# Hash-bucketed attention followed by two MLPs on one core: another order for the first pairs of heads, filler matmuls, late copies, and a last block stored tile by tile

## The chip, the cores and the metric

One core of one Trainium2 chip runs the whole kernel as one program. The metric is the device time of that core in microseconds. Times of single executions agree to about 0.1%; a time given here is the median of a few executions, and the profile comes from one more execution, with a time of its own.

The engines are called as the profile calls them: PE is TensorE (matmuls; PEld its weight loads), DVE is VectorE, ACT is ScalarE, POOL is GpSimd, SP is SyncE, whose queue issues nearly all the DMAs here. Each engine works through its own instructions in the order in which the program gives them, and waits on semaphores for the others.

## The reference

Inputs are `q`, `k`, `v` of shape (2, 8, 768, 64), a projection `proj` (64, 6) and two pairs of MLP weights, (512, 2048) and (2048, 512), all float32 (float64 in memory for the weights).

```
q_bits, k_bits = (q @ proj > 0), (k @ proj > 0)        # 6 bits a row: its bucket
scores = q @ k^T / 8;  scores[bucket(q) != bucket(k)] = -1e9
attn = softmax(scores);  x = attn @ v                  # 16 heads, 768 x 768 each
x = relu(x @ w_in)^2 @ w_out                           # 1536 tokens, 512 -> 2048 -> 512
g = h * tanh(softplus(h)), h = x @ w2_in;  out = g @ w2_out
```

Every float32 product is made of three products of float32r halves (high*high, high*low, low*high), so each matmul below comes in threes or with a second operand that carries the low halves.

## The kernel before

**Attention.** The 16 heads form 8 pairs. One step j (96 of them, N = 96, 12 to a pair, PER = 12) handles 128 queries of one head against all 768 keys. A step has, on PE: four score matmuls (`scores`, L365 and L367), six transposes of the exponentials (`transpose`, L392) and four matmuls with v for the group of three steps before (`pv`, L421). On DVE: `clamp` (L373, reads the scores from PSUM and takes the maximum) and `lower` (L409, low half of the transposed exponentials). On ACT: `exponent` (L382) and `upper` (L405, high half). Step j of the loop (L551 to L596) issues `scores(j+2)`, `exponent(j+1)`, `lower(j-1)`, `transpose(j)`, `clamp(j+2)`, `upper(j)`, a part of `pv`, in that order.

**PSUM.** `ps2` has three slots of two banks, taken in turn by scores, transposes and bits; `ps1` has two slots of one bank for the accumulators of `pv`. So scores and transposes of a step wait until DVE has emptied the slot they follow. The program puts the slots of `ps2` at banks 0, 4, 2 in turn and those of `ps1` at 6 and 7. After the attention the MLPs' pools take the same banks: hidden tiles (`psh`) at 4, 7, 6, 5 in turn, accumulators (`pacc`) at 0, 3, 2, 1.

**The next pair** is prepared inside the steps of the present one, by a plan (L483 to L499): `load` (q and k from memory), `split_q`, `split_k`, `split_v` on POOL (L311 to L346), `place_q`, `place_k` (three DMAs each, L321 and L339), and once a pair eight matmuls that make the hash bits (`bits_split`, L286), at the end of the step in `bits_at`. In the next step ACT negates one half of the bits (L291), DVE compares (L294), POOL scales (L295), and `place_bits` puts them below q and k by four DMAs (L304, L305). Calls of the plan run at the head of their step; the DMAs among them all go through SP's queue, one behind the other, each with its waits.

**Taking a group out.** After three steps of `pv` the accumulator is copied by ACT (`unstack`): for the first head of a pair to `hi` (L434), for the second to `both` (L439), a buffer of which there is one. Two DMAs (L442, L443, `place`) take `both` away a step later, behind all other calls of that step. `broadcast` (L450) copies the reciprocal sums out of PSUM (L453) and spreads them by DMAs (L461), `finish` (L465) on POOL adds and scales into `xf`. The first pair runs head by head, so that its two `both` come three steps apart; in the other pairs they come six steps apart.

**Weights.** `weights` (L86) converts float64 weights piece by piece. A piece is a fetch (512 KB), an absolute value (L117 on ACT in the attention), clamp and shift on DVE (L121, L122), two ORs on DVE (L124, L126) and two instructions on POOL (L127, L128). `next(conv)` takes one stage of it; `conv_at` names the steps that take one, at their end: 21 stages, five pieces, in the attention.

**The turn to the MLPs** (L597 to L626): the last sums are transposed into `rT`, the last `lower`, the ACT copies of `rT` and of accumulator 30, four `split` of the first block of tokens (L615 on ACT, L616 on DVE), twelve matmuls of the last `pv`, the last `unstack`.

**The MLPs** run as 8 weight groups by 3 blocks of 512 tokens by 4 chunks: `hidden` (L642 to L644, twelve matmuls), activation, and five steps later `down` (L688 to L696, twelve matmuls). `down` of the second MLP adds chunk fi to four accumulators (one for 128 tokens each); after the fourth chunk `collect` adds all four to `tot` on DVE (L710) and stores each by a DMA on SP (L713).

Of the kernel before, what the change touches and what calls it, by code (L numbers as in the profile page):

```python
# [17 lines left out]
P = 128  # L18
# [10 lines left out]
LAG = 5  # L29

WARM = 3

F64_LOW = 3.4332275390625e-05
# [4 lines left out]
def lsh_attention_relu2_mish_kernel(ctx, tc, qT, kT, vP, proj, w_in, w_out, w2_in, w2_out, out):  # L38
# [47 lines left out]
    def weights():  # L86
# [16 lines left out]
        for k, (i, nm, _, c) in enumerate(pieces):  # L103
# [11 lines left out]
            mu = m.bitcast(U32)  # L115
            if loaded[-1] == EXP_SET:
                nc.scalar.activation(m, hf, AF.Abs)  # L117
            else:
                nc.vector.scalar_tensor_tensor(m, hf, -1.0, hf, ALU.mult, ALU.max)
            yield  # L120
            nc.vector.tensor_scalar(m, m, F64_LOW, F64_HIGH, ALU.max, ALU.min)  # L121
            nc.vector.tensor_scalar(mu, mu, 3, 0x3FFFFFF8, ALU.logical_shift_left, ALU.bitwise_and)  # L122
# [25 lines left out]
    pm = early.enter_context(tc.tile_pool(name="pm", bufs=3))  # L148
    ps2 = early.enter_context(tc.tile_pool(name="ps2", bufs=3, space=PSUM))

# [208 lines left out]
    def scores(j):  # L359
        p, half, hh, t = seq[j]  # L360
        QA, QBt, KA, KBt = heads[p, hh]
        q0 = half * H2 + t * P
        ps = sc[j] = ps2.tile([P, 1024], F32, tag="ps2", name="s")
        for c0, c1 in ((0, 512), (512, S)):
            nc.tensor.matmul(ps[:, c0:c1], QA[:, q0:q0 + P], KA[:, c0:c1], start=True, stop=False)  # L365
        for c0, c1 in ((0, 512), (512, S)):
            nc.tensor.matmul(ps[:, c0:c1], QBt[:, q0:q0 + P], KBt[:, c0:c1], start=False, stop=True)  # L367
# [44 lines left out]
    def pv(g, n):  # L412

        p, half, hh, _ = seq[g * QT]
        if n == 0:
            accs[g] = ps1.tile([P, H2], F32, tag="ps1", name="acc")
# [8 lines left out]
    def unstack(g, j):  # L425
# [10 lines left out]
        else:  # L436
            hi, lo = hl[p, half]
            both = xt.tile([P, H2], F32, tag="both", name="both", bufs=1)
            nc.scalar.activation(both, acc, AF.Copy)  # L439
# [4 lines left out]

            at(j + 1, place)
            at(j + 4 + 2 * (j == N), lambda: finish(p, half))
# [32 lines left out]

    def at(j, f):  # L480
        calls.setdefault(j, []).append(f)

    bits_at = {}  # L483
    for p in range(NP - 1):
        o, n = p * PER, p + 1
        if p == 0:
            plan = ((3, split_q, (n,)), (4, split_k, (n,)), (5, place_q, (n, 0)), (6, place_k, (n, 0)),
                    (6, place_q, (n, 1)), (7, place_k, (n, 1)), (8, place_bits, (n, 0)), (8, place_bits, (n, 1)),
                    (8, split_v, (n,)), (8, load, (n + 1, "q_r")), (8, load, (n + 1, "k_r")), (11, load_v, (n + 1,)))
            bits_at[o + 6] = n  # L490
        else:
            plan = ((1, place_k, (n, 0)), (2, load, (n + 1, "q_r")), (3, load, (n + 1, "k_r")), (3, split_v, (n,)),
                    (7, place_bits, (n, 0)), (7, place_q, (n, 1)), (8, place_bits, (n, 1)), (8, place_k, (n, 1)),
                    (10, load_v, (n + 1,)))
            bits_at[o + 4] = n
# [4 lines left out]

    conv_at = [5, 6, 6, 8, 10] + [b for b in bits_at if b > PER for _ in range(2)] + [N - PER + m for m in (1, 4, 6, 8)]

# [43 lines left out]
    load(1, "q_r")  # L546
    load(1, "k_r")
    load_v(1)
    split_proj()
    waiting, bits, sums = None, None, None  # L550
    for j in range(N):  # L551
# [4 lines left out]
        if j + 1 < N:  # L556
            exponent(j + 1)
            sums = next((k for k, last in ends.items() if last == j + 1), None)
            if sums is not None:
                add_tiny(sums)  # L560
        if bits is not None:
            bits[0]()
        if waiting is not None:
            unstack(waiting, j)
            waiting = None
        if j:
            lower(j - 1)
        if bits is not None:
            bits[1]()
            bits = None  # L570
        if j == 1:
            head_qbits(1, 0, S, qb1)
        done = next(iter(r6s), None)
        transpose(j, r6s.get(done))
        if j + 2 < N:
            clamp(j + 2)
        if sums is not None:
            nc.vector.reciprocal(tiny[sums], tiny[sums])
            if j + 2 < N:
                r6s[sums] = tiny[sums]  # L580
            sums = None
        upper(j)
        if done is not None:
            del r6s[done]
            broadcast(*done, pts[j][:2 * QT, S:S + P], j)
        g, n = divmod(j, QT)
        if g:
            pv(g - 1, n)
            if n == QT - 1:
                waiting = g - 1  # L590
        if j == 0:
            qb1 = head_bits(1, 0, 0, S)
        if j in bits_at:
            bits = bits_split(bits_at[j])
        for _ in range(conv_at.count(j)):
            next(conv)  # L596
    for f in calls.pop(N, ()):  # L597
        f()
    ps = ps2.tile([P, 1024], F32, tag="ps2", name="rT")
    done = seq[N - 1][:2]  # L600
    r6 = tiny[done]
    nc.tensor.transpose(ps[:2 * QT, 0:P], r6, ident)
    lower(N - 1)
    broadcast(*done, ps[:2 * QT, 0:P], N)
    unstack(waiting, N)
    early.close()

# [10 lines left out]
    xs = {}  # L618
    split((0, 0), xf[0])
    for n in range(QT):  # L620
        pv(N // QT - 1, n)
    unstack(N // QT - 1, N)
# [77 lines left out]
    def collect(i, blk, acc):  # L700
# [13 lines left out]
        if layer == 0 and g == G - 1:  # L714
            split((1, blk), tot[blk])

    def retire(i, blk, fi, gh, gl):
        if fi == 0:
            acc[:] = [
# [68 lines left out]
```

## Time and profile before

| | |
|---|---|
| median of 3 runs | 762.97 us (762.72 to 763.20) |
| the profiled execution's own time | 762.05 us |
| its span | 759.9 us |
| PE busy | 745.8 us, 98% of the span |
| DVE, ACT, POOL busy | 534.5, 358.0, 263.9 us |
| chain that ended last | PE 86%, DMA 4%, DVE 3%, ACT 2%, POOL 2%, issue 2% |

The span goes from the first to the last recorded instruction; 2.15 us of the execution lie around it. A chain is followed back from the last instruction to whatever released it. In a row of the timeline the columns are start, length, engine, line, operation, operands, count, and in brackets the idle time before it with what ended it.

### The profile page before, as it was taken

To read this page: it belongs to the slowest core of one execution; us is meant where nothing else is said; L and a number is where in the kernel's file an instruction comes from. 1 tells how busy PE (TensorE), PEld (TensorE's weight loads), DVE (VectorE), ACT (ScalarE), POOL (GpSimd) and SP (SyncE) were. 2 spreads that over 40 slices of the span, in tenths; PEclk is the share of its full clock that TensorE was granted. 3 is DMA by queue.
4 is the path that set the end of the run, shared out by engine and by line. 5 is a ranking of instruction groups with operands and counts; after the bars stand their busy time and mean duration, and the time that the engine had idled before them with its cause. 6 is when DMAs were issued, how large, how long until landed. Compare 5 with 4: busy or idle time off the path is not lost.

```text
span 759.9 us, 10509 instructions
## 1 busy us (share of the span) xinstructions
PE 745.8 (98%) x3742; PEld 635.5 (84%) x3742; DVE 534.5 (70%) x859; ACT 358.0 (47%) x640; POOL 263.9 (35%) x261
## 2 busy tenths in 40 slices
PE   8889999999999999999999999999999999999997
PEld 4779999999998888888888888888888888888886
DVE  8878988988997966566566688978454767566223
ACT  6878889889897443423233213333223121212120
POOL 9464555655223433232232232224223222232100
PEclk9999999999999999999999999999999999999999
DMA  5775696678423122122121122112212111120013
GB/s 145 196 207 157 167 232 158 167 203 193 108 71 92 56 84 82 57 69 70 56 84 55 56 68 67 60 56 84 84 55 81 59 56 56 56 83 28 1 55 111
DMA packets 28956, 72.69 MB, mean 96 GB/s; under 512 B 5048, under 2 KB 10264, under 8 KB 28904
## 3 DMA queue, kind: packets, MB, share of 16 engines
q1 hardware_dynamic: 28824, 72.01, 33.5%
q8 instruction: 30, 0.49, 0.3%
q14 instruction: 22, 0.18, 0.1%
q10 hardware_dynamic: 80, 0.00, 0.0%
HBM read 46.14 MB, written 3.19 MB: 65 GB/s over the span
## 4 chain that ended last, share of the span: by engine, by line
PE 86%; DMA 4%; DVE 3%; ACT 2%; POOL 2%; issue 2%; SPq 0%; DVEq 0%; ACTq 0%; POOLq 0%
PE h L642 11%; PE h L644 11%; PE h L643 11%; PE pT L392 6%; PE acc L421 6%; PE acc L688 6%; PE acc L689 6%; PE acc L690 6%; PE acc L696 6%; PE acc L695 6%; PE acc L694 6%; PE s L367 3%; PE s L365 3%; DVE pl L409 1%; ACT ph L405 1%
## 5 line engine op out<-in xcount | busy, mean ns | idle before, releaser
L643 PE MATMUL h<-xs,wi 128*128 128x512 f32 x384 | 149.4, 389 | 0.0
L644 PE MATMUL h<-xs,wi 128*128 128x512 f32 x384 | 149.4, 389 | 0.0
L642 PE MATMUL h<-xs,wi 128*128 128x512 f32 x384 | 149.4, 389 | 0.0
L668 ACT ACTIVATE g<-h 128x512 f32<-128x512 f32 x48 | 28.7, 598 | 188.7 <-PE h L644 172.0
L409 DVE TENSOR_TENSOR pl<-pT,ph 128x768 fp32r<-128x768 f32 x96 | 91.7, 956 | 20.1 <-ACT ph L405 13.4
L652 ACT ACTIVATE r<-h 128x512 f32<-128x512 f32 x48 | 28.7, 598 | 153.3 <-PE h L644 153.3
L127 POOL TENSOR_SCALAR wo<-cv 128x512 fp32r<-128x512 f32 x32 | 29.4, 918 | 194.3 <-DVE cv L126 178.9
L382 ACT ACTIVATE e<-e,nm 128x768 f32<-128x768 f32 x96 | 89.8, 936 | 6.0 <-DVE e L373 5.5
L673 DVE TENSOR_TENSOR gl<-g,gh 128x512 fp32r<-128x512 f32 x48 | 35.9, 748 | 80.6 <-ACT gh L670 80.6
L373 DVE TENSOR_SCALAR_CACHE_REDUCE e<-s 128x768 f32<-128x768 f32 x96 | 91.0, 947 | 0.9 <-PE s L367 0.8
L654 DVE TENSOR_TENSOR s<-r 128x512 f32<-128x512 f32 x48 | 38.8, 808 | 70.2 <-ACT r L652 70.2
L405 ACT ACTIVATE ph<-pT 128x768 fp32r<-128x768 f32 x96 | 77.7, 809 | 18.2 <-PE pT L394 10.1
L644 PEld LDWEIGHTS h<-xs,wi 128*128 128x128 f32 x384 | 72.1, 188 | 15.1
L642 PEld LDWEIGHTS h<-xs,wi 128*128 128x128 f32 x384 | 72.1, 188 | 14.9
L643 PEld LDWEIGHTS h<-xs,wi 128*128 128x128 f32 x384 | 72.0, 188 | 14.8
L392 PE MATMUL pT<-ident,e 128*128 128x128 f32 x576 | 79.1, 273 | 3.6 <-DVE pl L409 3.2
L127 POOL TENSOR_SCALAR wi<-cv 128x512 fp32r<-128x512 f32 x32 | 27.3, 854 | 147.5 <-DVE cv L126 147.5
L392 PEld LDWEIGHTS pT<-ident,e 128*128 128x128 f32 x576 | 66.3, 140 | 11.2 <-ACT r L386 1.9
L688 PE MATMUL acc<-gh,wo 128*128 128x512 f32 x192 | 74.7, 389 | 0.0
L689 PE MATMUL acc<-gl,wo 128*128 128x512 f32 x192 | 74.7, 389 | 0.0
L690 PE MATMUL acc<-gh,wo 128*128 128x512 f32 x192 | 74.7, 389 | 0.0
L694 PE MATMUL acc<-wo,gh 128*128 128x512 f32 x192 | 74.7, 389 | 0.0
(111 smaller groups left out, 1413.8 us busy)
## 6 DMA issues: line engine op xcount, KB each, us to landing
stg<-in_w_in_dram SPq DMA_DIRECT2D x32, 512.0 KB
stg<-in_w_out_dram SPq DMA_DIRECT2D x32, 512.0 KB
KA<-kh SPq DMA_DIRECT2D x28, 192.0 KB
v_r<-in_vP_dram SPq DMA_DIRECT2D x8, 384.0 KB
rb<-rd SPq DMA_DIRECT2D x32, 96.0 KB
out_dram<-tot SPq DMA_DIRECT2D x12, 256.0 KB
q_r<-in_qT_dram SPq DMA_DIRECT2D x7, 384.0 KB
k_r<-in_kT_dram SPq DMA_DIRECT2D x7, 384.0 KB
```

The costliest lines, as they stand in the source:

```text
L373: nc.vector.tensor_scalar(e, ps[:, 0:S], MASKED, None, ALU.min, ALU.min, accum_out=nm)
L382: nc.scalar.activation(e, e, AF.Exp, bias=nm, scale=-1.0, accum_out=ssums[p, half][:, c:c + 1])
L392: nc.tensor.transpose(ps[:, c * P:(c + 1) * P], e[:, c * P:(c + 1) * P], ident)
L405: nc.scalar.activation(ph, v, AF.Copy)
L409: nc.vector.tensor_tensor(pl, v, b32(ph), ALU.subtract)
L642: nc.tensor.matmul(h, w[:, 0, fi, cs], xs[:, 0, c, :], start=c == 0, stop=False)
L643: nc.tensor.matmul(h, w[:, 0, fi, cs], xs[:, 1, c, :], start=False, stop=False)
L644: nc.tensor.matmul(h, w[:, 1, fi, cs], xs[:, 0, c, :], start=False, stop=c == PPB - 1)
L688: nc.tensor.matmul(y, w[:, 0, fi, cs], gh, start=fi == 0, stop=False)
L689: nc.tensor.matmul(y, w[:, 0, fi, cs], gl, start=False, stop=False)
L690: nc.tensor.matmul(y, w[:, 1, fi, cs], gh, start=False, stop=fi == FC - 1)
L694: nc.tensor.matmul(o, gh[:, qs], w[:, 0, fi, :], start=fi == 0, stop=False)
```

## The change

- The plan of the first pair is re-ordered: the loads of pair 2 go from step 8 to step 4, bits from step 6 to 5, `place_k(1, 0)` and both `place_bits` one step earlier, `place_k(1, 1)` one later, `load_v` from 11 to 9. For the second pair (p = 1) the loads go from steps 14 and 15 to 16 and 17.
- `conv_at` is another list of the same 21 stages, one of which (the first fetch) runs before step 0. In a step the stage now comes after `lower(j-1)` and ahead of compare, transposes and `clamp`.
- For pieces 1 to 4 the absolute value and its clamp are three POOL instructions, in place of one on ACT and one on DVE.
- `scores(0)` gets two matmuls with a tile of zeros (`FILL`) between its first and second pair of matmuls.
- `place` of `both` goes to the head of its step's calls.
- The end of the attention: `clamp(95)` comes one step earlier (ahead of `lower(92)`), the copies out of accumulators 29 and 30 come after the loop, between and behind the `split`s; the last sums are made on DVE; the copy of the transposed sums (now `rp`) comes after all `split`s; the last `pv` accumulates in a slot of `ps2`, which therefore stays open until the end of the attention.
- The last block's `down` of the second MLP: chunks are kept, and after the fourth each 128-token tile gets its twelve matmuls in a row, its addition and its DMA; the last tile is done in two halves of 256 columns, the second half stored through ACT's queue.

```diff
+EARLY = 5
+FILL = 2
...
-            if loaded[-1] == EXP_SET:
+            if 0 < k < EARLY:
+                nc.gpsimd.tensor_scalar(m, hf, 0.0, -2.0, ALU.min, ALU.mult)
+                nc.gpsimd.tensor_tensor(m, m, hf, ALU.add)
+                nc.gpsimd.tensor_scalar(m, m, F64_LOW, F64_HIGH, ALU.max, ALU.min)
+            elif loaded[-1] == EXP_SET:
                 nc.scalar.activation(m, hf, AF.Abs)
...
-            nc.vector.tensor_scalar(m, m, F64_LOW, F64_HIGH, ALU.max, ALU.min)
+            if not 0 < k < EARLY:
+                nc.vector.tensor_scalar(m, m, F64_LOW, F64_HIGH, ALU.max, ALU.min)
...
-    ps2 = early.enter_context(tc.tile_pool(name="ps2", bufs=3, space=PSUM))
+    ps2 = late.enter_context(tc.tile_pool(name="ps2", bufs=3, space=PSUM))
...
+        for _ in range(FILL * (j == 0)):
+            nc.tensor.matmul(ps[:, 0:H2], zero[:, 0:P], zero, start=False, stop=False)
...
-            both = xt.tile([P, H2], F32, tag="both", name="both", bufs=1)
+            if g < N // QT - 1:
+                both = xt.tile([P, H2], F32, tag="both", name="both", bufs=1)
+            else:
+                both = b32(pt.tile([P, KT, H2], F32R, tag="ph", name="both")[:, 0, :])
...
-            at(j + 1, place)
+            at(j + 1, place, j < N)
...
-    def at(j, f):
-        calls.setdefault(j, []).append(f)
+    def at(j, f, first=False):
+        c = calls.setdefault(j, [])
+        c.insert(0 if first else len(c), f)
...
-            plan = ((3, split_q, (n,)), (4, split_k, (n,)), (5, place_q, (n, 0)), (6, place_k, (n, 0)),
-                    (6, place_q, (n, 1)), (7, place_k, (n, 1)), (8, place_bits, (n, 0)), (8, place_bits, (n, 1)),
-                    (8, split_v, (n,)), (8, load, (n + 1, "q_r")), (8, load, (n + 1, "k_r")), (11, load_v, (n + 1,)))
-            bits_at[o + 6] = n
+            plan = ((3, split_q, (n,)), (4, split_k, (n,)), (4, load, (n + 1, "q_r")), (4, load, (n + 1, "k_r")),
+                    (5, place_q, (n, 0)), (5, place_k, (n, 0)), (6, place_q, (n, 1)), (7, place_bits, (n, 0)),
+                    (7, place_bits, (n, 1)), (8, place_k, (n, 1)), (8, split_v, (n,)), (9, load_v, (n + 1,)))
+            bits_at[o + 5] = n
         else:
-            plan = ((1, place_k, (n, 0)), (2, load, (n + 1, "q_r")), (3, load, (n + 1, "k_r")), (3, split_v, (n,)),
+            m = 2 if p > 1 else 4
+            plan = ((1, place_k, (n, 0)), (m, load, (n + 1, "q_r")), (m + 1, load, (n + 1, "k_r")), (3, split_v, (n,)),
...
-    conv_at = [5, 6, 6, 8, 10] + [b for b in bits_at if b > PER for _ in range(2)] + [N - PER + m for m in (1, 4, 6, 8)]
+    conv_at = [4, 6, 6]
+    for p in range(1, NP - 1):
+        conv_at += [p * PER + m for m in ((4, 6) if p % 2 else (4, 5))]
+    conv_at += [N - PER - 4, N - PER - 3] + [N - PER + m for m in (2, 3, 6)]
...
     load(1, "k_r")
+    next(conv)
     load_v(1)
...
-        if waiting is not None:
+        if waiting is not None and j < N - QT:
             unstack(waiting, j)
             waiting = None
+        if j == N - 3:
+            clamp(j + 2)
+        if j == N - 1:
+            done = seq[j][:2]
+            r6 = sm.tile([P, 2 * QT], F32, tag="r6", name="r6", bufs=2)
+            nc.vector.tensor_scalar(r6, ssums.pop(done), 1e-9, None, ALU.add)
+            nc.vector.reciprocal(r6, r6)
         if j:
             lower(j - 1)
+        for _ in range(conv_at.count(j)):
+            next(conv)
         if bits is not None:
             bits[1]()
             bits = None
...
-        if j + 2 < N:
+        if j + 3 < N:
             clamp(j + 2)
...
-        for _ in range(conv_at.count(j)):
-            next(conv)
-    for f in calls.pop(N, ()):
-        f()
-    ps = ps2.tile([P, 1024], F32, tag="ps2", name="rT")
-    done = seq[N - 1][:2]
-    r6 = tiny[done]
-    nc.tensor.transpose(ps[:2 * QT, 0:P], r6, ident)
+    rp = ps2.tile([P, 1024], F32, tag="ps2", name="rT")[:2 * QT, 0:P]
+    nc.tensor.transpose(rp, r6, ident)
     lower(N - 1)
-    broadcast(*done, ps[:2 * QT, 0:P], N)
-    unstack(waiting, N)
+    accs[N // QT - 1] = ps2.tile([P, 1024], F32, tag="ps2", name="acc")[:, 0:H2]
+    for n in range(QT):
+        pv(N // QT - 1, n)
     early.close()
...
-    split((0, 0), xf[0])
-    for n in range(QT):
-        pv(N // QT - 1, n)
+    split((0, 0), xf[0], 0, 2)
+    unstack(waiting, N - 1)
+    for f in calls.pop(N):
+        f()
+    split((0, 0), xf[0], 2)
+    unstack(N // QT - 2, N)
+    broadcast(*done, rp, N)
     unstack(N // QT - 1, N)
...
+    def last(blk, kept):
+        w = W[2 * G - 1, "o"]
+        nt = TB // P
+        for t in range(nt):
+            qs = slice(t * P, (t + 1) * P)
+            o = pacc.tile([P, DM], F32, tag="acc", name="acc")
+            n = 1 + (t == nt - 1)
+            for h in range(n):
+                cs = slice(h * DM // n, (h + 1) * DM // n)
+                for fi, (gh, gl) in enumerate(kept):
+                    nc.tensor.matmul(o[:, cs], gh[:, qs], w[:, 0, fi, cs], start=fi == 0, stop=False)
+                    nc.tensor.matmul(o[:, cs], gh[:, qs], w[:, 1, fi, cs], start=False, stop=False)
+                    nc.tensor.matmul(o[:, cs], gl[:, qs], w[:, 0, fi, cs], start=False, stop=fi == FC - 1)
+                x = tot[blk][:, t, cs]
+                nc.vector.tensor_tensor(x, x, o[:, cs], ALU.add)
+                r0 = blk * TB + t * P
+                (nc.scalar if h else nc.sync).dma_start(out=out[r0:r0 + P, cs], in_=x)
...
     def retire(i, blk, fi, gh, gl):
+        if (i, blk) == (2 * G - 1, NBLK - 1):
+            kept.append((gh, gl))
+            if fi == FC - 1:
+                last(blk, kept)
+            return
```

## Rows read from the trace of the kernel before

**Rows 1.** Waits of PE: what waited for what, total us, times, longest.
```profile
PE pT L392 <- DVE pl L409: 3.2, 6, 1.6
PE bits L286 <- POOL xf L474: 3.2, 1, 3.2
PE s L367 <- DVE QB L262: 1.2, 1, 1.2
PE s L365 <- DVE pl L409: 0.6, 1, 0.6
```

**Rows 2.** Timeline of PE, steps 39 to 41: start, length, engine, line.
```profile
106.89 0.82 PE L392 MATMUL pT<-ident,e 128*128 128x128 f32 x6
...
108.94 0.82 PE L392 MATMUL pT<-ident,e 128*128 128x128 f32 x6
...
110.30 0.51 PE L286 MATMUL bits<-qh,pwr 128*112 128x512 f32 x2
...
111.70 0.51 PE L365 MATMUL s<-KA,QA 128*128 128x512 f32 x2
...
113.09 0.85 PE L392 MATMUL pT<-ident,e 128*128 128x128 f32 x6 [0.54 <-DVE pl L409]
```

**Rows 3.** Timelines of PE, ACT, DVE and POOL, 26 to 37 us.
```profile
26.06 0.82 PE L392 MATMUL pT<-ident,e 128*128 128x128 f32 x6
...
31.27 0.84 PE L392 MATMUL pT<-ident,e 128*128 128x128 f32 x6 [1.60 <-DVE pl L409]
...
28.66 0.67 ACT L117 ACTIVATE cv<-stg 128x512 f32<-128x512 f32 x1 [0.94 <-DMA stg<-in_w_in_dram]
...
34.92 1.76 DVE L124 SCALAR_TENSOR_TENSOR cv<-stg,cv 128x512 uint32<-128x512 uint32 x1
...
34.28 1.85 POOL L346 TENSOR_TENSOR vs<-v_r,vs 128x768 fp32r<-128x768 f32 x1
```

**Rows 4.** Groups by line and form: count, busy us, mean ns, idle before.
```profile
L124 DVE SCALAR_TENSOR_TENSOR cv<-stg,cv 128x512 uint32<-128x512 uint32 x64 | 45.0, 704 | 1.0
...
L128 POOL TENSOR_TENSOR wi<-cv,wi 128x512 fp32r<-128x512 f32 x32 | 43.4, 1356 | 2.7
...
L208 PE MATMUL zeros<-zero 128*128 128x384 f32 x6 | 4.1, 857 | 1.3 <-DVE zero L184 1.3
...
L222 PE MATMUL bits<-k,pw 128*76 128x512 f32 x4 | 2.0, 592 | 0.0
```

**Rows 5.** Timelines of PE, ACT, SP and POOL, 40 to 60 us.
```profile
51.02 0.82 PE L392 MATMUL pT<-ident,e 128*128 128x128 f32 x6
...
59.16 1.14 PE L392 MATMUL pT<-ident,e 128*128 128x128 f32 x6
...
53.42 0.49 ACT L439 ACTIVATE both<-acc 128x384 f32<-128x384 f32 x1 [3.90 <-DMA lo<-both]
...
48.95 0.82 SPq L443 DMA_DIRECT2D lo<-both  x1
...
40.40 1.12 POOL L311 TENSOR_SCALAR qh<-q_r 128x768 fp32r<-128x768 f32 x1 [4.27 <-DMA q_r<-in_qT_dram]
```

**Rows 6.** Stretch 58 to 60 us: busy time of each engine, PEclk, DMA share, GB/s.
```profile
58.00:60.00 2.00, 2.00 (x10) 1.80 (x10) 1.79 (x3) 0.81 (x1) 0.00 (x0) 0.55 0.44 160
```

**Rows 7.** Timelines of ACT and PE, 229 to 234 us.
```profile
229.81 1.64 ACT L405 ACTIVATE ph<-pT 128x768 fp32r<-128x768 f32 x2
231.44 0.27 ACT L453 ACTIVATE rs<-rT 6x128 f32<-6x128 f32 x1
...
231.98 2.18 ACT L615 ACTIVATE xs<-xf 128x512 fp32r<-128x512 f32 x4
...
233.70 0.39 PE L642 MATMUL h<-xs,wi 128*128 128x512 f32 x1
```

**Rows 8.** Timeline of DVE from 752 us.
```profile
754.11 2.73 DVE L710 TENSOR_TENSOR tot<-tot,acc 128x512 f32<-128x512 f32 x4 [8.15 <-PE acc L696]
```

**Rows 9.** DMA rate in 40 equal slices of 753 to 760 us.
```profile
GB/s 0 0 0 0 0 0 0 0 0 0 0 0 0 0 0 257 410 386 351 363 386 386 351 387 398 374 375 375 398 410 339 47 0 0 0 0 0 0 0 0
```

More of the change, by code (lines that the diff above doesn't have):

```diff
@@ L414, in pv @@
         p, half, hh, _ = seq[g * QT]
-        if n == 0:
+        if n == 0 and g not in accs:
             accs[g] = ps1.tile([P, H2], F32, tag="ps1", name="acc")
@@ L557, in lsh_attention_relu2_mish_kernel @@
             exponent(j + 1)
-            sums = next((k for k, last in ends.items() if last == j + 1), None)
+            sums = next((k for k, last in ends.items() if last == j + 1 < N - 1), None)
             if sums is not None:
@@ L572, in lsh_attention_relu2_mish_kernel @@
             head_qbits(1, 0, S, qb1)
-        done = next(iter(r6s), None)
-        transpose(j, r6s.get(done))
-        if j + 2 < N:
+        ready = next(iter(r6s), None)
+        transpose(j, r6s.get(ready))
+        if j + 3 < N:
             clamp(j + 2)
@@ L578, in lsh_attention_relu2_mish_kernel @@
             nc.vector.reciprocal(tiny[sums], tiny[sums])
-            if j + 2 < N:
-                r6s[sums] = tiny[sums]
+            r6s[sums] = tiny[sums]
             sums = None
         upper(j)
-        if done is not None:
-            del r6s[done]
-            broadcast(*done, pts[j][:2 * QT, S:S + P], j)
+        if ready is not None:
+            del r6s[ready]
+            broadcast(*ready, pts[j][:2 * QT, S:S + P], j)
         g, n = divmod(j, QT)
@@ L588, in lsh_attention_relu2_mish_kernel @@
             pv(g - 1, n)
-            if n == QT - 1:
+            if n == QT - 1 and j < N - 1:
                 waiting = g - 1
@@ L715, in collect @@
             split((1, blk), tot[blk])
-    def retire(i, blk, fi, gh, gl):
+    def last(blk, kept):
[15 more added lines that the diff above has]
+                (nc.scalar if h else nc.sync).dma_start(out=out[r0:r0 + P, cs], in_=x)
+    kept = []
+    def retire(i, blk, fi, gh, gl):
+        if (i, blk) == (2 * G - 1, NBLK - 1):
[3 more added lines that the diff above has]
+            return
         if fi == 0:
```

## The prediction

> **What bounds the kernel now.** I read the page first: PE is busy for 98% of the span and carries 86% of the chain of waits. The MLPs hold two thirds of that and show no wait of PE, so the change can only gain where PE stands still: in the attention, at the turn to the MLPs and after the last matmul. So I read the waits of PE next [rows 1]: it waits for DVE's `lower` (L409) seven times, 3.8 us together; besides, once 3.2 us ahead of the bits (where the row names POOL), and 1.2 us at the start for DVE's QB. Then PE's timeline, step by step: the reader is to see a pace, 108.94 - 106.89 = 2.05 us a step, and bits that take 111.70 - 110.30 = 1.40 us [rows 2]. A step with bits should so take 3.45 us. Whatever is longer is to be had; whatever keeps PE at this pace is worth nothing.
>
> **First pair, steps 6 to 10.** The step with bits took 31.27 - 26.06 = 5.21 us, 1.76 too many [rows 3]. ACT waited 0.94 us for the first fetch of weights, its absolute value (L117) came late, DVE's clamp stood behind it, and `lower` behind that. A second wait, 0.57 us, is [rows 1]'s last; it stands behind a single L124 of 1.76 us where the mean is 0.70 [rows 3, 4]. In [rows 2] a step with a wait of 0.54 lost 4.15 - 3.45 = 0.70, so a restart costs 0.16. Together 1.76 + 0.57 + 0.16 = 2.5 us. After the change the fetch is issued before step 0, some 9 us ahead of its use, and L126 leaves this stretch. Not all goes: bits are now in step 5, and stage b (clamp, shift) and c (L124) both come in step 6, ahead of compare and of `clamp(8)` on DVE; I take 0.3 for that, between 0 and one L124 more, 0.7. Gain 2.2.
>
> **Second pair, steps 16 and 17.** 59.16 - 51.02 = 8.14 us against 3.45: 4.69 lost, and the transposes at 59.16 took 1.14 us instead of 0.82, since the granted clock had fallen to 0.55, the lower of its levels [rows 5, 6]: 5.0 in all. The row of PE names POOL; but POOL's `xf` has nothing that the bits read, and `lower`, which empties the slot that the bits need, ended at the same time. The cause is on ACT: `both` waited 3.90 us for the DMA that takes the former `both` away, issued at 48.95 [rows 5]. That was late because SP stood behind `place_k(2, 0)`, which waited for `split_k(2)` on POOL, which began late since q of pair 2 came at 40.40, 4.27 us after POOL was free for it [rows 5]. The change takes two links out: the loads of pair 2 go out at step 4, and `place` goes to the head of step 13. I follow SP's queue: the loads of step 4 need the buffers of head 1, free after its bits at about 15 us; they leave at 17 or 18 us; each issue takes some 0.6 us; `both` of group 2 is then issued at about 42 us and needs, by its landing in 4.5 us (48.95 to 53.42) at worst, until 46.5; group 3's `both` is due about 47. So 4.8 gained, 0.2 kept for the L126 in this step; bounds: 1.9 (a landing 3 us later than this) and 5.0. With the loads of pair 3 going to steps 16 and 17, nothing of this stretch stands behind them; they are first used at step 21, 10 us later.
>
> **The five later bits.** Seven waits of `lower` less the two above leave 3.8 - 1.6 - 0.57 = 1.6 us [rows 1]; with five restarts of 0.16, 2.4. In each, two stages of conversion stood between the recip and `lower` on DVE, just where `transpose` waits for it. Now one stage comes before `clamp`, the other in the next step between `lower` and compare, where DVE waits for ACT's negation anyway, or two steps later. What stays is the chain bits, negation, compare, `clamp`: worked through on the step of [rows 2] it ends 0.1 to 0.2 us too late. Five times 0.14: 0.7 kept, 1.7 gained; bounds 0.5 and 2.4. Outside these steps, stages now come at steps 80, 81, 86, 87 and 90 instead of 85 to 92: an L124 or L126 of 0.70 [rows 4] against a slack of some 0.5 us ahead of `clamp`; I take -0.1 for step 80, the others cancel.
>
> **POOL.** Three more instructions a piece, four pieces. No row has an absolute value on POOL; the nearest is L128's 1.36 us, so up to 4.1 us a piece [rows 4], at least 0. They come at steps 18, 42, 66 and 81 and are wanted 5 to 10 steps, over 10 us, later; the POOL work queued behind them (`finish`, then the next `split_q` three steps later) has that time too. Cost 0.
> Here a rule speaks against the change. In [rows 3] L124 took 1.76 us while POOL's L346 ran from 34.28 to 36.13. The Trainium skill, SBUF — State Buffer, "Who interferes with whom", says that a DVE instruction with two SBUF inputs and a GpSimd instruction that reads SBUF exclude each other, the later one being held until the other ends. The trace agrees: 36.13 and one L124 give 36.8, it ended at 36.68. By this every L124 or L126 that meets a POOL instruction is held; that result is the second rival.
>
> **Filler.** Three such calls were six instructions of 0.86 us at the very start, 4.1 us in all, 0.69 from start to start [rows 4]. Two calls are four, so 2.7 us by that. But float32 matmuls of 512 columns a little later (L222) took 0.59 [rows 4], so 384 columns take 0.44 there, and start to start, in the same proportion, 0.35: 1.4 us, beside the 1.2 us in which PE waits for QB [rows 1]. Cost 0.2; bounds 0 and 1.5. No row shows that the clock fell in that gap, so I count no gain.
>
> **The turn to the MLPs.** Here I expect a loss. `rp` lies in the second slot of `ps2`, bank 4, and the first hidden tile is put in bank 4 too; so its first matmul waits until ACT has copied `rp`. Before, that copy came right behind the last `upper`, 231.44 to 231.71, and PE began at 233.70 without waiting [rows 7]. Now ACT does four `split` copies (2.18) and two accumulators (0.49 each, [rows 5]) first: 231.45 + 2.18 + 0.98 + 0.27 = 234.9, less 0.1 of overlap for each instruction, 234.4; its signal 0.1. The earlier `clamp(95)` delays `lower(92)` by up to one DVE instruction (the nearest, L124, takes 0.70 [rows 4]) and brings the last `exponent` forward: I take 0.3 late for the last `upper`. 234.8 - 233.7 = 1.1 lost; bounds 0 and 1.7. The activation and `down` of the MLPs shift with it and change nothing.
>
> **The end.** The four additions run 754.11 to 756.84, 0.68 each [rows 8]; DMA moves 1 MB from slice 15 (755.6) to slice 31 (758.45) without a pause [rows 9], and the span ends 1.45 later. Afterwards three tiles have left by then. The last half is added by 756.5 (PE ends about 756.1), starts moving 0.85 later, as the first tile did, and takes 0.35 at that rate: 757.7, gain 0.75. Halves cost PE 0 to 0.1: four pairs of 512 and 256 columns took 1.40 [rows 2], the same for each column. ACT's queue has issued no such DMA here; I take 0.5, bounds 0 and 0.9.
>
> **Sum.** 2.2 + 4.8 + 1.7 - 0.1 - 0.2 - 1.1 + 0.5 = 7.8 us. From the profiled execution's 762.05: 754.25; it lies 0.92 below the median of the runs. For a median like that one, 762.97 - 7.8 = 755.2.
>
> **Rivals.**
> 1. The turn costs nothing (the copy isn't waited for) and residues are small: 1.1 + 0.8 more, 753.3. For it: PE's last `pv` ends no earlier than 233.8 anyway. Against: the bank. 12%.
> 2. DVE's two-input stages meet POOL: L126 at step 16 meets `finish`, those at 28 to 77 meet `split_v` (which ran up to the step of the bits), each held about 1.1 us (1.76 - 0.70). Two or three of them in steps with bits: 2.5 us, 757.7. Against: in the step of [rows 2] DVE gets there, as I count it, 0.2 us after POOL is done. The rule cited above gives this time. 13%.
> 3. The change doesn't free `both`: its DMAs still land late, since POOL or the queue lags elsewhere; 3.5 of the 4.8 stay. 758.7. For it: group 3 has half a microsecond to spare. 8%.
> 4. Slower: the loads of pair 2 (2 x 384 KB), with two fetches, now go ahead of the copies that `scores(12)` needs (`place_q(1, 0)`, `place_k(1, 0)`, `place_bits(1, 0)`). I have the last landing at about 34 us, PE there at about 35.5. Every microsecond beyond is PE's. From 9.3 us late on (1.5 to spare and the 7.8) the change loses; at 12 late it costs 10.5, 765.7. Against: 1.8 MB at the 375 GB/s of [rows 9] is 5 us, and they leave at 18. 7%.
>
> The forecast itself, 753.6 to 757.0 by its terms, gets 60%. Such a kernel tells changes of 0.2%, 1.5 us, from none. All cases but the fourth, and a mixture of 2, 3 and a dear filler that I give 5% for no change, are faster: faster 0.87, same 0.05, slower 0.08. 752.0 to 759.0 leaves out the fourth rival, the worst of the third and luck beyond the first: under 2 in 10.
>
> **What would show it.** Right: PE's wait for `xf` and ACT's for `lo<-both` are gone, the PE clock doesn't fall around 55 us; steps with bits at 3.45 to 3.7 us; a new wait of `h` L642 for ACT's `rs`, about 1 us; DMA after the last matmul under 2 us. Wrong: a wait of `s` L365 for a DMA at step 10, DVE's L124 or L126 above 1 us, a bits step above 4 us, or no new wait at the turn.

## The result

The changed kernel takes 756.35 us (median of 5 runs, 755.91 to 757.22) against 762.97 (762.32 to 764.67) for the kernel before: a ratio of 0.9913, 95% interval 0.9899 to 0.9927. That is 6.6 us faster where 7.8 was forecast. Single executions of one kernel differ by 0.2 to 0.3% here, not by about 0.1%. The profiled execution took 756.32 us, its span is 754.5, so profile against profile the gain is 762.05 - 756.32 = 5.7.

The page of the changed kernel, first its engines, then the chain that ended last:

```profile
PE 747.5 (99%) x3758; PEld 635.1 (84%) x3758; DVE 532.8 (71%) x857; ACT 356.4 (47%) x635; POOL 284.7 (38%) x273
...
PE 96%; DVE 2%; ACT 1%; issue 1%; ACTq 0%
```

PE's share of the chain rose from 86% to 96%, and POOL and DMA have left it. POOL is busy for 20.8 us more than before, which costs nothing that the chain shows. Waits of PE, the same view as [rows 1]:

```profile
PE zeros L217 <- DVE zero L193: 1.3, 1, 1.3
PE h L670 <- ACT rs L467: 0.6, 1, 0.6
PE acc L756 <- DVE tot L760: 0.5, 1, 0.5
PE s L374 <- DVE q_r L303: 0.4, 2, 0.3
PE s L374 <- DVE QB L271: 0.2, 1, 0.2
PE pT L403 <- DVE e L384: 0.2, 1, 0.2
```

The rows of [rows 1] are gone: the seven waits for `lower`, the 3.2 us that named `xf`, and of the 1.2 us for QB all but 0.2. Two new ones of half a microsecond are at the turn (`h`) and at the end (`acc`); two small ones are for compare (L303) and `clamp` (L384). The first row, 1.3 us, was there before. Now PE's timeline over the step with bits that answers to [rows 2]:

```profile
100.89 0.82 PE L403 MATMUL pT<-ident,e 128*128 128x128 f32 x6
...
102.94 0.82 PE L403 MATMUL pT<-ident,e 128*128 128x128 f32 x6
...
106.39 0.82 PE L403 MATMUL pT<-ident,e 128*128 128x128 f32 x6
...
108.83 0.88 PE L403 MATMUL pT<-ident,e 128*128 128x128 f32 x6
```

From start to start of the transposes: 2.05 us without bits, 106.39 - 102.94 = 3.45 with them, exactly the pace that the forecast took for the ideal (it was 4.15). The step behind it takes 2.44 instead of 2.20: part of what was in the way has only moved on. In the first pair, answering to [rows 3], and then around the second pair's bits, answering to [rows 5] (PE, ACT, SP, DVE and POOL):

```profile
24.60 0.81 PE L403 MATMUL pT<-ident,e 128*128 128x128 f32 x6
...
28.05 0.82 PE L403 MATMUL pT<-ident,e 128*128 128x128 f32 x6
...
30.59 0.87 PE L403 MATMUL pT<-ident,e 128*128 128x128 f32 x6
```

```profile
49.34 0.81 PE L403 MATMUL pT<-ident,e 128*128 128x128 f32 x6
...
52.99 0.88 PE L403 MATMUL pT<-ident,e 128*128 128x128 f32 x6
...
47.74 0.47 ACT L453 ACTIVATE both<-acc 128x384 f32<-128x384 f32 x1
...
43.77 0.59 SPq L457 DMA_DIRECT2D lo<-both  x1
...
33.45 0.84 POOL L320 TENSOR_SCALAR qh<-q_r 128x768 fp32r<-128x768 f32 x1
...
49.86 1.27 DVE L135 SCALAR_TENSOR_TENSOR cv<-stg,cv 128x512 uint32<-128x512 uint32 x1
...
49.57 1.01 POOL L483 TENSOR_TENSOR hi<-hi,lo 128x384 f32<-128x384 f32 x1
```

The step with bits took 3.45 us in the first pair (5.21 before) and 3.65 in the second (8.14). POOL starts on q of pair 2 at 33.45 instead of 40.40, SP issues `lo<-both` at 43.77 instead of 48.95, and ACT's next `both`, at 47.74, waits for nothing. The clock stays up: the stretch that answers to [rows 6], with the same columns, has a granted clock of 1.00 (2.4 GHz) instead of 0.55.

```profile
52.00:54.00 2.00, 2.00 (x15) 1.59 (x14) 1.00 (x4) 1.84 (x3) 1.87 (x3) 1.00 0.62 225
```

The groups that answer to [rows 4]: POOL's three new instructions, four pieces.

```profile
L121 POOL TENSOR_SCALAR cv<-stg 128x512 f32<-128x512 f32 x4 | 7.9, 1986 | 0.0
L123 POOL TENSOR_SCALAR cv<-cv 128x512 f32<-128x512 f32 x4 | 7.7, 1928 | 0.4
L122 POOL TENSOR_TENSOR cv<-cv,stg 128x512 f32<-128x512 f32 x4 | 5.3, 1314 | 0.3
```

The turn, ACT and PE, answering to [rows 7]:

```profile
226.17 1.15 ACT L639 ACTIVATE xs<-xf 128x512 fp32r<-128x512 f32 x2
227.21 0.48 ACT L445 ACTIVATE hi<-acc 128x384 f32<-128x384 f32 x1
227.58 0.25 ACT L467 ACTIVATE rs<-rT 6x128 f32<-6x128 f32 x1
...
227.88 0.50 PE L670 MATMUL h<-xs,wi 128*128 128x512 f32 x1 [0.58 <-ACT rs L467]
```

The end, DVE and PE, answering to [rows 8], and the DMA rate in 40 slices of 747 to 755 us, answering to [rows 9]:

```profile
747.75 0.69 DVE L760 TENSOR_TENSOR tot<-tot,acc 128x512 f32<-128x512 f32 x1 [2.03 <-PE acc L758]
749.18 0.42 DVE L760 TENSOR_TENSOR tot<-tot,acc 128x256 f32<-128x256 f32 x1 [0.74 <-PE acc L758]
751.39 0.42 DVE L760 TENSOR_TENSOR tot<-tot,acc 128x256 f32<-128x256 f32 x1 [1.79 <-PE acc L758]
...
749.66 0.39 PE L756 MATMUL acc<-wo,gh 128*128 128x256 f32 x1 [0.51 <-DVE tot L760]
```

```profile
GB/s 410 123 0 0 0 0 0 0 0 0 0 184 369 369 359 31 0 189 358 108 0 0 0 0 0 0 0 0 133 348 174 0 0 0 0 0 0 0 0 0
```

The first half of the last tile was added at 749.18, the second only at 751.39, 2.21 later, though its twelve matmuls take about 1.4; between them PE waits for the first addition. The last half's data are through at about 753.2 (slice 30), and the span ends 1.3 us later.

The gain by stretches, from the starts of the transposes in both timelines (plus is time won): up to the first transposes -0.59; steps 6 to 11 +2.27; steps 16 to 19 +4.10; the five later steps with bits and the two behind each +1.45; steps 80 to 92 -1.0 (81, 87, 88 and 91 above all); from step 93 to the first `h` -0.4; from there to the end of the span -0.4. Together 5.4, the difference of the spans (759.9 - 754.5).

### The profile page after: what moved, and what is told of

The parts are those of the page before. It is cut to its first block, busy times and chain, and to the rows that moved or that the text cites. A ratio compares the mean times of both kernels' runs of the same rounds, so it can differ in the third digit from the quotient of the medians.

```text
span 754.5 us, 10568 instructions
## 1 busy us (share of the span) xinstructions
PE 747.5 (99%) x3758; PEld 635.1 (84%) x3758; DVE 532.8 (71%) x857; ACT 356.4 (47%) x635; POOL 284.7 (38%) x273
## 4 chain that ended last, share of the span: by engine, by line
PE 96%; DVE 2%; ACT 1%; issue 1%; ACTq 0%
PE h L670 12%; PE h L672 12%; PE h L671 12%; PE acc L432 8%; PE pT L403 8%; PE acc L716 6%; PE acc L718 6%; PE acc L717 6%; PE acc L724 5%; PE acc L723 5%; PE acc L722 5%; PE s L374 4%; PE s L378 4%; PE bits L295 1%; DVE e L384 1%
## 5 line engine op out<-in xcount | busy, mean ns | idle before, releaser
L136 POOL TENSOR_SCALAR wo<-cv 128x512 fp32r<-128x512 f32 x32 | 29.5, 921 | 196.1 <-DVE cv L135 180.8
L384 DVE TENSOR_SCALAR_CACHE_REDUCE e<-s 128x768 f32<-128x768 f32 x96 | 90.9, 947 | 1.6 <-PE s L378 1.5
L136 POOL TENSOR_SCALAR wi<-cv 128x512 fp32r<-128x512 f32 x32 | 27.4, 856 | 144.7 <-DVE cv L135 144.7
L722 PE MATMUL acc<-wo,gh 128*128 128x512 f32 x176 | 68.5, 389 | 0.0
```

Source lines behind the costliest of these rows:

```text
L384: nc.vector.tensor_scalar(e, ps[:, 0:S], MASKED, None, ALU.min, ALU.min, accum_out=nm)
L722: nc.tensor.matmul(o, gh[:, qs], w[:, 0, fi, :], start=fi == 0, stop=False)
```

## The experiments

All are edits of the changed kernel. A time is of one run unless a median is given. The kernel before took 762.39, 761.09 and (median of 7) 763.2 us beside the three groups in which these runs were made, so whole times of single runs differ by up to 2 us without a cause in the kernel. What an edit does is therefore read from the steps that it touches. A step's length is from the transposes before to its own; in steps that an edit does not touch it agrees within 0.1 us, but for step 87 (see below).

**Which link held `both`.** The change took two links out; each is put back alone, then both.

```diff
 e4_place_last
-            at(j + 1, place, j < N)
+            at(j + 1, place)
 e5_loads_step8
-            plan = (..., (4, split_k, (n,)), (4, load, (n + 1, "q_r")), (4, load, (n + 1, "k_r")), ...)
+            plan = (..., (8, split_v, (n,)), (8, load, (n + 1, "q_r")), (8, load, (n + 1, "k_r")), ...)
 e45_both_links_back: both edits
```

> The changed kernel, but place of both stays behind the other calls of its step. Theory (the early loads of pair 2 alone empty SP's queue): step 16 to 17 stays at 3.7 us, ACT's wait of both for lo<-both stays 0, span within 0.3 of 754.5. Rival (the head of the step is what frees both): ACT's second both waits 1 to 4 us, step 16 to 17 takes 5 to 8 us, span 756 to 759.

> The changed kernel, but the loads of pair 2 go back from step 4 to step 8; place stays at the head of its step. Theory (the early loads are the link that counts): POOL waits 2 to 4 us for q of pair 2 again, split_k(2) ends late; but place(13) no longer stands behind place_k(2, 0), so both is still freed in time and the step 16 to 17 stays under 4 us: span 754 to 755.5. Rival (both links are needed): ACT's second both waits over 1 us, step 16 to 17 takes over 4.5 us, span over 756.

> The changed kernel with both links undone: loads of pair 2 at step 8 and place behind the other calls. Theory (the chain load, split_k, place_k, place, both made the 5 us): ACT's both waits 2 to 4 us for lo<-both and the step 16 to 17 takes 5.5 to 8 us, span 756.5 to 759. Rival (something else in the re-ordered plan, such as bits a step earlier, made the gain): the step stays under 4.5 us, span under 756.

757.59, 757.55 and 762.11 us. In the first two my theory, that one link alone keeps step 17 under 4 us, fell, and the rival came. Step 17 takes 5.31 us with `place` last, 5.11 with the loads late, 9.66 with both (3.65 in the changed kernel). ACT's `both` in the third:

```profile
52.51 0.49 ACT L453 ACTIVATE both<-acc 128x384 f32<-128x384 f32 x1 [4.88 <-DMA lo<-both]
```

With one link back that wait is 2.16 or 1.97 us; in the changed kernel it is none. SP issues `lo<-both` at 45.36 us in the first, 47.57 in the second and 49.25 in the third, against 43.77 in the changed kernel. So the cause that the forecast read behind the row naming `xf` is shown: with both links back the whole stall returns, 6.0 us of step 17, and `xf` has not been touched. (Step 17 is even longer than the 8.14 us of the kernel before: PE reaches it 1.9 us earlier, `both` comes free only 0.9 earlier.) The links are not additive, 1.66 + 1.46 against 6.0: either edit alone would have brought most of the gain, since SP gets past `place_k(2, 0)` early or `place` no longer stands behind it.

**Absolute value off POOL again.**

```diff
-EARLY = 5
+EARLY = 1
```

> The changed kernel, with the absolute values and clamps of pieces 1 to 4 back on ACT and DVE (no POOL instructions for them). Theory (POOL's part is hidden and spares DVE little): POOL 21 us less busy, DVE 1.7 more, steps with bits as before within 0.2 us each, span 754.3 to 755.5. Rival (the spared ACT and DVE time is what shortened the steps with bits): the five later bits steps lose 0.3 us each again, span 756 or more.

759.09 us. My theory fell, and so did the rival's place: steps with bits stay as they were, but steps 20, 30, 44, 54, 68, 78, 83 and 87 take 2.42 to 2.63 us instead of 2.05 to 2.28, 3.3 us in all with the steps behind them, and no step is shorter than in the changed kernel. Two causes share this. ACT and DVE in step 20:

```profile
56.60 0.66 ACT L125 ACTIVATE cv<-stg 128x512 f32<-128x512 f32 x1
...
57.99 0.96 DVE L420 TENSOR_TENSOR pl<-pT,ph 128x768 fp32r<-128x768 f32 x1 [0.99 <-ACT ph L416]
```

Here, and in steps 44, 68 and 83, the absolute value stands on ACT ahead of `upper`, and `lower` waits 0.99 us for `upper`: 0.49 us a step. In steps 30, 54, 78 and 87 it is the clamp that came back to DVE (L130, 0.42 us), ahead of DVE's `clamp` of the scores: 0.17 to 0.35 us a step. On POOL, where nobody waits for it, the same work is three instructions of 5.2 us together (the groups above) and costs PE nothing. The longer way around is the cheaper one.

**The end.** The second half gets a PSUM tile of its own; or the last tile is not cut.

```diff
 e1_half_own_bank
             for h in range(n):
+                if h:
+                    o = pacc.tile([P, DM], F32, tag="acc", name="acc")
 e2_whole_tile
-            n = 1 + (t == nt - 1)
+            n = 1
```

> The changed kernel, but the second half of the last tile accumulates in a PSUM tile of its own. Theory (the second half waited for the addition of the first because both lie in one PSUM tile): PE's wait of 0.5 us for that addition goes, the last matmul ends 0.6 us earlier relative to the first of the last block, span 753.9 (0.6 less). Rival (PE's gap is a cost of the narrow matmuls or of the turn of columns): the gap stays, span 754.5.

> The changed kernel with the last tile whole, 512 columns, one addition, one DMA of 256 KB. Theory (halves as written lose the 0.64 us wait and 0.2 us of narrow matmuls, and give back 0.27 us of addition and some 0.35 us of DMA): span 754.2 to 754.5, no worse than the halves. Rival (the halves give more at the DMA than they cost): span 755 or more.

755.09 and 755.74 us, against 756.32 for the changed kernel; but the first `h` starts 0.45 and 0.31 us earlier here, far ahead of the edit. From the first `h` to the end of the span it is 525.87 us with the tile of its own, 526.33 uncut, 526.62 in the changed kernel and 526.20 in the kernel before. Both theories held. With its own tile PE's wait is gone and the halves are added 1.43 us apart instead of 2.21:

```profile
748.72 0.42 DVE L762 TENSOR_TENSOR tot<-tot,acc 128x256 f32<-128x256 f32 x1 [0.75 <-PE acc L760]
750.15 0.42 DVE L762 TENSOR_TENSOR tot<-tot,acc 128x256 f32<-128x256 f32 x1 [1.01 <-PE acc L760]
```

Uncut, the last addition ends at 750.86 and the span 3.04 us later. In the kernel before it ended at 756.84, and the span 3.06 later [rows 8]. So three tiles that left earlier help nothing (3.04 against 3.06): before, the additions came every 0.68 us and a tile of 256 KB needs about 0.70 at the rate of [rows 9]; the queue never had a tile in hand. What gains is the half (2.69 and 2.73 from its addition to the end): with a tile of its own it is 0.46 us better than the uncut tile. As the change makes it, it pays 0.75 for the shared tile and ends up 0.29 worse than no cut. The new tile also lies in another bank; whether tile or bank is what the wait goes by was not separated.

**The copy of `rp` ahead of the splits.**

```diff
+    broadcast(*done, rp, N)
     split((0, 0), xf[0], 0, 2)
 ...
     unstack(N // QT - 2, N)
-    broadcast(*done, rp, N)
```

> The changed kernel with the copy of the transposed sums (rp) moved ahead of the first split on ACT. Theory (the first hidden tile waits for that copy, as both lie in bank 4): PE's wait of 0.58 us of h for ACT's rs goes, PE starts the MLPs 0.5 us earlier relative to the last transposes; a new wait for the first split of at most 0.2; span 754.0. Rival (the first hidden tile would wait for the splits anyway): the wait stays at 0.4 us or more with another name, span 754.5.

755.17 us. From the last transposes to the first `h` 3.91 us instead of 4.69 (3.98 before), and `h` waits for nothing. So the copy of `rp` is what `h` waited for, and not the splits; 0.78 us was the price. That it did so for the bank which both share is read from the program's placement; no run moved the bank alone.

**Stages of the last steps behind `clamp`.** From step 80 on a stage comes at the end of its step.

```diff
-        for _ in range(conv_at.count(j)):
+        for _ in range(conv_at.count(j) * (j < N - PER - 4)):
             next(conv)
 ...
+        for _ in range(conv_at.count(j) * (j >= N - PER - 4)):
+            next(conv)
```

> The changed kernel, but the stages of steps 80 to 90 run at the end of their step, behind clamp, as they did before the change. Theory (a stage ahead of clamp uses up the 0.45 us that the next transposes have to spare): steps 81, 87, 88 and 91, 2.25 to 2.37 us in the changed kernel, come back to 2.05 to 2.16, 0.5 to 0.9 us in all, span 753.7 to 754.0. Rival (DVE simply has too much to do in these steps, wherever the stage stands): they lose the same 1.0 us in other steps, span 754.5.

755.45 us. Steps 81, 87, 88 and 91 take 2.05 or 2.06 us; in the changed kernel they took 2.27, 2.25, 2.35 and 2.37, 1.0 us more together. Of this the 0.2 of step 87 is not the order's: an L131 took 0.70 us there beside POOL's L488, where its mean is 0.46, and in e4, e5 and e10, with the stage in the same place, step 87 takes 2.05. That leaves 0.8. How a stage costs there, DVE of the changed kernel:

```profile
214.63 0.68 DVE L135 SCALAR_TENSOR_TENSOR cv<-stg,cv 128x512 uint32<-128x512 uint32 x1
215.23 0.95 DVE L384 TENSOR_SCALAR_CACHE_REDUCE e<-s 128x768 f32<-128x768 f32 x1
```

L135 runs between `lower` and `clamp` (L384), and `clamp` starts 0.6 us later than it could; in steps 81, 88 and 91 0.22 to 0.32 of that reaches PE.

**No filler.**

```diff
-FILL = 2
+FILL = 0
```

> The changed kernel without the two matmuls of zeros. Theory (they lie wholly in PE's wait for QB and neither cost nor keep up anything): from DVE's compare of QB to the first transposes as in the changed kernel within 0.1 us, granted clock 1.0 in both, span 754.2 to 754.8. Rival (they hold the clock or delay the scores): the first transposes move by 0.3 us or more against that compare, or the clock falls in the first 20 us.

756.96 us. My theory, that the filler keeps nothing up, fell. PE waits 1.91 us for QB, and the granted clock over 8 to 14 us, the last number but two of the row, is 0.76, between its two levels. First this kernel, then the changed one:

```profile
8.00:14.00 6.00, 4.17 (x13) 2.56 (x13) 4.53 (x8) 3.30 (x6) 5.70 (x15) 0.76 0.38 78
```

```profile
8.00:14.00 6.00, 5.90 (x27) 3.73 (x26) 5.07 (x9) 3.09 (x5) 5.70 (x15) 1.00 0.38 76
```

The wait and what PE did behind it, without the filler:

```profile
9.83 0.58 PE L378 MATMUL s<-KB,QB 128*128 128x512 f32 x2 [1.91 <-DVE QB L271]
...
10.96 2.60 PE L231 MATMUL bits<-k,pw 128*76 128x512 f32 x4
```

Those four bits matmuls take 2.60 us instead of 1.45, and the first transposes come at 14.59 instead of 13.52. In the kernel before the gap was 1.2 us and those matmuls took 1.45.

The filler itself costs nothing: in the changed kernel as in the kernel before, PE's next scores start 0.15 us after the compare of QB ends. What it buys depends on how early PE is. The kernel with three fixes (below) compares QB at the same time as this one (9.08 and 9.07 us) and has the filler: its wait is 0.60 us, its clock 1.00, its first transposes come at 13.22, so 1.4 us are won. In the changed kernel's own profile PE came later; without the filler its gap would have been about 1.2 us (8.94 to 10.14), as long as the one that left the clock up before. There a gain is not shown.

**One stage out of `finish`'s way.** The stage of step 16 goes to step 14.

```diff
+    conv_at[conv_at.index(PER + 4)] = PER + 2
```

> The changed kernel with one stage (L135 of the first piece) moved from step 16 to step 14. Theory (at step 16 it was held 0.6 us by POOL's finish, and that made the two steps after it long): L135 takes 0.68 us instead of 1.27, step 17 comes from 3.65 to 3.45 to 3.5, step 18 from 2.82 to 2.3 to 2.5; step 15 may lose 0.2; span 754.0. Rival (the chain bits, negation, compare, clamp makes these steps long without any stage): they stay at 3.6 and 2.8, span 754.5.

755.74 us. Steps 17 and 18 fall from 3.65 and 2.82 to 3.45 and 2.29, step 15 rises from 2.06 to 2.23: 0.56 gained. At its new place L135 takes 0.68 us; at the old one it took 1.27, beside POOL's L483. Steps 41 and 42, where an L135 stands in the same place of its pair and takes 0.68, last 3.45 and 2.44 us: so of the 0.73 won in steps 17 and 18, 0.58 is the price of being held, and 0.15 that of the stage itself.

**Three fixes together**, e1, e3 and e6, and **all stages moved**, those three with every stage behind `clamp` and the earlier stages in ordinary steps.

```diff
 best2_stages_moved
-    conv_at = [4, 6, 6]
+    conv_at = [4, 8, 9]
 ...
-        conv_at += [p * PER + m for m in ((4, 6) if p % 2 else (4, 5))]
+        conv_at += [p * PER + m for m in ((2, 6) if p % 2 else (2, 3))]
 ...
```

> The changed kernel with three edits together: own PSUM tile for the last half, the copy of rp ahead of the first split, the stages of steps 80 to 90 behind clamp. If the three gains (0.6, 0.6 to 0.8, 1.0) add up: span 752.2 to 752.4, some 2.2 us below the changed kernel, median 754.0 to 754.4. If they meet in one place (the turn takes what step 91 gives): 1.4 us, 755.

> As the kernel with three edits, and every stage at the end of its step, none in a step with bits or in the one after: first pair 4, 8, 9, odd pairs o+2 and o+6, even pairs o+2 and o+3. Theory (a stage costs nothing behind clamp in an ordinary step, as steps 80 to 90 show, and 0.1 to 0.6 in the steps with bits): steps 7, 18, 42 and 66 lose 0.1 to 0.2 instead of 0.28 to 0.66, together 1 to 1.7 us, span 750.6 to 751.4. Rival (those steps are set by negation and compare alone): as the other kernel, span 752.2 to 752.4.

The three fixes take **753.62 us** (median of 4, 753.23 to 753.95), a ratio to the kernel before of 0.987 (0.9853 to 0.9886), outside the changed kernel's interval: the version that beats both. Its span is 751.6, 2.9 less than the changed kernel's: 1.0 in the steps (0.2 of it step 87), 0.75 at the turn, 0.8 at the end and 0.3 at the start, which no fix touches. Alone the three had won 0.8 (and step 87), 0.78 and 0.75 at the same places, so they add up.

All stages moved gives 757.24 (median of 4, 757.0 to 757.72; ratio 0.9917, 0.9902 to 0.9932), 3.6 worse than that and no better than the changed kernel; 0.8 of the 3.6 is a later start. Steps 29, 53 and 77 take 4.06 to 4.10 us instead of 3.45, step 10 3.80 instead of 2.05. DVE and POOL at step 29 of this kernel:

```profile
77.48 1.52 DVE L133 SCALAR_TENSOR_TENSOR cv<-stg,cv 128x512 uint32<-128x512 uint32 x1
...
76.61 1.84 POOL L355 TENSOR_TENSOR vs<-v_r,vs 128x768 fp32r<-128x768 f32 x1
```

L133 took 1.52 us (mean 0.69) while L355 ran until 78.45; at 35.10 an L131 took 1.95 (mean 0.46) beside POOL's L321, 34.65 to 36.77. My theory, that a stage behind `clamp` of an ordinary step is free, fell: which POOL instruction it meets decides. Steps 7, 17, 18, 42 and 66 did gain, 0.15 to 0.5 each.

## Why the prediction came out right

The forecast's mechanism held and its largest terms were sized well. In its own terms the spans gave 5.4 of 7.8 us: the second pair, the later bits, the stages, the start and the end fell short by 3.2 together, and the turn and the first pair came out 0.8 better than forecast, so part of the match is luck. Two small terms, stages and end, make most of the difference. The cause is shown by experiments for the second pair, the turn, the stages of the last steps and the end. For the first pair and the five later steps no run puts the old order back; there it is read from the rows.

- **First pair, +2.2:** +2.27. The residue was 0.49, in step 7 (2.54), for which 0.3 was taken. The clamp, the shift and the first OR (L130, L131, L133) run there from 27.20 to 28.80, ahead of compare, as foreseen. Moved to later steps, they leave 0.24 (2.29, all stages moved).
- **Second pair, +4.8:** +4.10. The cause was `both`, as argued, and the two links were the right ones (e45). The 0.2 kept for L126 (now L135) was too little: it ran 1.27 us beside POOL's L483, and steps 17 and 18 keep 0.2 and 0.77 above pace. e10 wins 0.56 of it back. An L124 or L126 above 1 us was one of the forecast's signs of being wrong, and this one came: it is the second rival, at one of the places that it named and with a part of its price; at the steps of the later bits, its other places, the changed kernel shows 3.45 us.
  The Trainium skill, SBUF — State Buffer, "Who interferes with whom", which the forecast cited for it, fits the ends, which lie one free length behind POOL's: L483 ended at 50.58 and a free L135 (0.70) later is 51.28, it ended at 51.13; L355 at 78.45 plus 0.69 is 79.14, that L133 ended at 79.00.
- **Five later bits, +1.7:** +1.45. The steps with bits are at 3.45, better than the 0.14 residue each; the two steps behind each pay 0.06 to 0.25.
- **Stages outside, -0.1:** -1.0, the term most mis-sized. The forecast counted them at one step and said that the others cancel. The same stages in the same steps, but behind `clamp`, cost nothing (e6); ahead of it they use more than the slack of half a microsecond. The order within the step, not the number of the step, was the price of 0.8; the other 0.2 is the longer L131 of step 87, beside POOL's L488.
- **POOL, 0:** 0 on PE, but 5.2 us a piece, above the 4.1 given as the upper bound. That the work leaves ACT and DVE is worth 3.3 us in this order (e7), which the forecast did not see: about 2.0 for ACT's part and 1.2 for DVE's. It sits in the steps that did not get longer.
- **Filler, -0.2; start -0.59:** the filler itself costs nothing (e8). The first transposes come 0.59 us late since DVE's first compare of bits starts at 7.35 us instead of 6.75, and ahead of it PE's four bits matmuls took longer, first in the kernel before, then in the changed one:

```profile
5.26 1.45 PE L222 MATMUL bits<-k,pw 128*76 128x512 f32 x4
```

```profile
5.32 1.99 PE L231 MATMUL bits<-k,pw 128*76 128x512 f32 x4
```

  In the eleven other kernels of this document that keep the filler, these four take 1.45 to 2.51 us and the first transposes come at 13.01 to 14.04, so much of the 0.59 is scatter from run to run, which the forecast did not count. ACT's first copy waited 1.66 us for the projection, 0.18 before; but that is not what decides: in e5 and e6 it waits 0 and 0.18, and the first transposes come at 13.54 and 13.63. Why PE is slower there in some runs stays open; the granted clock of these stretches is 1.00 in all of them.
- **Turn, -1.1:** -0.4 net. The wait was there, for the copy that was named. ACT's part came out as worked out: from the end of the last `upper` (224.86) to the end of `rs` (227.83) 2.97 us, where the forecast had 234.4 - 231.45 = 2.95; PE began 3.02 after that `upper`, 2.25 before, so 0.77 was lost. What was off is the 0.3 by which the last `upper` should have come late: step 95 took 0.29 less instead. e3 shows that the loss could be spared.
- **End, +0.5:** -0.4, the wrong sign. The tail from the last matmul's end to the span's end did shorten, from 3.78 to 3.14, near the 0.75 forecast. But PE ended late: "halves cost PE 0 to 0.1" overlooked that both halves lie in one PSUM tile, so the second half's first matmul waited for the addition that reads the first, about 0.8 us of pace with the restart (e1); narrow matmuls add 24 x 0.12 - 12 x 0.227 = 0.16.

The rivals: the turn at no cost (1) did not come; the second came at one place (above); `both` not freed (3) did not come; the slower one (4) neither, since `scores(12)` at step 10 runs at 2.05 us with no wait for a DMA.

## What to carry to other kernels

When a wait names one producer, look for another that ends at the same time, follow its queue back, and put the suspected links back one by one and together: here either alone left 1.5 us and both 6.0. Ask of each moved instruction not only in which step it runs but what stands behind it in its engine's order and what the neighbour engine runs at that moment. Two halves of one tile are one tile to whoever waits for it; give each its own before counting on overlap.

## What was not expected of the hardware

- POOL's `tensor_scalar` with minimum or maximum took 1.93 to 1.99 us for 128x512 float32 (L121, L123), while the multiply-add one of the same size (L136) takes 0.86 to 0.92 on average, and its two-input operation 1.31.
- An L131 on DVE, with one input, took 1.95 us instead of 0.46 beside POOL's L321, as the two-input ones do beside POOL; another took 0.70 beside L488 (step 87).
- A PE gap of 1.2 us near the start left the granted clock at 1.00; one of 1.91 us at the same place, in another run, was followed by a fall, 0.76 over 8 to 14 us.
- A 256 KB store ended the span 3.04 us after its addition when the tiles before had left, 3.06 when it was the last of four in a row; half the size ended it 2.7 after.
